# New numbers for the open experts before each search, fewer packed sums, and TensorE's order as written in the expert loop

## The chip, the cores and the metric

The kernel runs on one core of a Trainium2 chip. The metric is the device time of one execution in microseconds (us). A core has engines with an instruction stream each: TensorE (PE in the profile, its weight loads PEld), VectorE (DVE), ScalarE (ACT), GpSimd (POOL) and SyncE (SP), and 16 DMA engines that move data.

## The reference, cut to what matters

```python
y = irfft(rfft(x, axis=1) * (filt_r + 1j * filt_i), axis=1)       # x: 8 x 3072 x 256
t = y.reshape(24576, 256)
t = np.maximum(np.maximum(t @ w1, t @ w2), t @ w3) @ w_out        # first stage
logits = t @ w_gate                                               # 24576 x 8, second stage
for idx in argsort(-logits.flatten()):
    tok, e = idx // 8, idx % 8
    if assigned[tok] >= 0 or counts[e] >= 3072: continue          # 24576 / 8
    assigned[tok] = e; counts[e] += 1
for e in range(8):
    out[assigned == e] = relu(t[assigned == e] @ W1[e]) @ W2[e]    # 256 -> 1024 -> 256
```

Every expert ends with exactly 3072 tokens.

## The kernel before, in words

The filter and the first stage fill the time to about 2157 us of the profiled span and are not touched. The second stage never sorts. Each token claims the open expert on which its logit is greatest (`best` holds the logit, `code` the expert's number, 8 for expert 0 down to 1 for expert 7). The expert that is filled next is the one whose 3072nd-best claim is the highest, and its tokens are the claims above that threshold. `pick(j)` finds both. It searches the threshold bit by bit, from bit 30 down, with 33 counts in all; a count asks, for a trial threshold and all experts at once, how many claims reach it. The counts of three experts share one float32: `W[k]` holds, for each token, 1, 256 or 65536 by the expert that it claims, and one VectorE instruction (`ck`, line 828) makes the masked sum over a partition's 192 tokens. Three such sums make the eight counts. Two conversions (lines 833 and 834) take the packed words apart into bytes, a TensorE matmul with ones (line 836) adds the bytes over the partitions, and a compare (line 866) tells whether any expert reaches 3072. The next trial follows from it, so a search is a ring through VectorE and TensorE. Behind the search two small steps settle ties; `weights` starts the DMA of the found expert's weights and then splits them into high and low halves; `slots` turns the selection into token numbers: a running sum (line 703), three matmuls, and then six blocks of four matmuls each into two PSUM tiles `pg` (line 734), after which VectorE makes two masked sums for each tile (`jk`, line 744) and the numbers `ids` (line 748); a compare `G` (line 720) prepares the next block. `between(j)` is `clear(j)`, which takes the filled expert and its tokens out, and `prepare(j + 1)`, which makes the claims and the words `W` anew.

The work itself is a loop of 8 experts `j` by 48 steps `i`: six groups of 512 tokens by eight slices of the hidden layer. A step is six matmuls of 128x512 into `hq` (three products of float32 halves for each of two depths), a ScalarE relu `qh` (line 1016), a VectorE residual `ql` (line 1017), and, one step late, twelve matmuls of 128x256 into `yp`. Tokens come by indirect DMA, `gather`, are transposed on TensorE (`xt`, line 931, two times four transposes a group) and split into `xh` and `xl`; results leave by indirect DMA from GpSimd (line 961). `xt` and `pg` share one PSUM pool of two buffers. Line numbers 77 and 78 are the helper that splits into halves, 82 to 84 the helper that issues the three products.

The search and the slots for the next expert run beside an expert's steps. The generator `side` is advanced once a step: `pick(j + 1)` in steps 0 to 42, `between(j + 1)` from step 43 (`SWITCH`) on. Each `yield` in these functions is thus a step's end. In the first expert, `side` is the rest of the first pick, then `between(0)`, then `pick(1)`, and it is advanced twice in the steps 0 to 6. Ahead of the loop the string `START` advances the first weights (w), the first gather (g) and the first pick (s).

Where nothing else is said, a planner orders each engine's instructions by its own costs. Inside `tc.manual_schedule(engines=set(MAN))`, with `MAN` TensorE alone, TensorE takes its instructions in the order in which the program issues them. Before the change this holds for the part ahead of the loop, in which the first pick runs beside the last blocks of the first stage.

Of the kernel before, what the change touches and what calls it, by code (L numbers as in the profile page):

```python
# [59 lines left out]
E = 8  # L60
# [569 lines left out]
def phase2(tc, X2, M, first_claims, e8, Woh, Wol, H, wa, wb, pos16, tabs, ident, out):  # L630
# [4 lines left out]
    with ExitStack() as ctx:  # L635
# [38 lines left out]
        def small(n, name, dt=F32):  # L674
            return rp.tile([128, n], dt, tag=name, bufs=2, name=name)
# [25 lines left out]
        def slots(j, sel, rs):  # L701
            scan = rp.tile([128, NTT], F16, tag="scan", name=f"scan{j}")
            v.tensor_tensor_scan(
                out=scan, data0=one1.to_broadcast([128, NTT]), data1=sel, initial=0.0, op0=ALU.mult, op1=ALU.add
            )
            pd = ranks
            nc.tensor.matmul(pd[:, NTT : NTT + 1], shift, rs, start=True, stop=True)
            nc.tensor.matmul(pd[:, NTT + 2 : NTT + 3], tri, rs, start=True, stop=True)
# [41 lines left out]
                yield  # L750

        prep = {}
        loads = []
        chosen = {}

# [3 lines left out]
        def prepare(j):  # L759
            if j == E - 1:  # L760
                return
            m = best
            eq = rp.tile([128, NTT, E], F16, tag="eq", name=f"eq{j}")
            code = rp.tile([128, NTT], F32, tag="code", name=f"code{j}")
            for t in pieces():
                n = NTT // NS
                v.tensor_reduce(out=m[:, t], in_=M[:, t], axis=AX.X, op=ALU.max)
                v.scalar_tensor_tensor(out=m[:, t], in0=alive[:, t], scalar=-NEG, in1=m[:, t], op0=ALU.mult, op1=ALU.min)
                v.tensor_tensor(
                    out=eq[:, t], in0=M[:, t], in1=m[:, t].unsqueeze(2).to_broadcast([128, n, E]), op=ALU.is_equal  # L770
                )
                if NY > 1:
                    yield
                v.tensor_tensor(out=eq[:, t], in0=eq[:, t], in1=e8h.unsqueeze(1).to_broadcast([128, n, E]), op=ALU.mult)
                v.tensor_reduce(out=code[:, t], in_=eq[:, t], axis=AX.X, op=ALU.max)
                if NS < 4 or (t.start // (NTT // NS)) % 2:
                    yield
            W = rp.tile([128, 3, NTT], F32, tag="W", name=f"W{j}")
            for e in range(E):
                k, f = divmod(e, 3)  # L780
                dst = W[:, k, :]
                if f:
                    dst = rp.tile([128, NTT], F32, tag="pen", bufs=2, name=f"pen{j}_{e}")
                v.tensor_scalar(
                    out=dst, in0=code, scalar1=float(E - e), scalar2=float(256**f), op0=ALU.is_equal, op1=ALU.mult
                )
                if f:
                    v.tensor_tensor(out=W[:, k, :], in0=W[:, k, :], in1=dst, op=ALU.add)
            prep[j] = m, code, [W[:, k, :] for k in range(3)]
            yield  # L790

        def clear(j):
            if j == E - 1:
                return
            sel, oh = chosen.pop(j)
            v.scalar_tensor_tensor(out=alive, in0=sel, scalar=-2.0, in1=alive, op0=ALU.mult, op1=ALU.add)
            v.tensor_tensor(out=open_, in0=open_, in1=oh, op=ALU.subtract)
            v.tensor_scalar(out=oh, in0=oh, scalar1=2.0 * NEG, scalar2=-NEG, op0=ALU.mult, op1=ALU.add)
            for t in pieces():
                v.tensor_tensor(  # L800
                    out=M[:, t], in0=M[:, t], in1=oh.unsqueeze(1).to_broadcast([128, NTT // NS, E]), op=ALU.min
                )
            yield

        def pick(j):
            if j == E - 1:
# [12 lines left out]
                yield from slots(j, sel, rs)  # L819
                return  # L820
            m, code, W = prep.pop(j)

            def count(thr):

                pk = small(3, "pk")
                for k in range(3):
                    jk = rp.tile([128, NTT], F16, tag="ck", bufs=2, name=f"ck{j}")
                    v.scalar_tensor_tensor(
                        out=jk, in0=m, scalar=thr, in1=W[k], op0=ALU.is_ge, op1=ALU.mult,
                        accum_out=pk[:, k : k + 1],  # L830
                    )
# [5 lines left out]
                return ranks[:, :12]  # L837

# [12 lines left out]
            v.tensor_scalar(out=pos, in0=neg, scalar1=1, scalar2=None, op0=ALU.bitwise_xor)  # L851
            for b in range(30, -1, -1):
                pc = yield from count(tr.bitcast(F32))
                nx = small(1, "nx", I32)
                v.tensor_scalar(out=nx, in0=tr, scalar1=(1 << b) >> 1, scalar2=None, op0=ALU.bitwise_xor)
                met = small(1, "met", I32)
                v.scalar_tensor_tensor(
# [6 lines left out]
                hit = small(12, "hit")  # L864
                any_ = small(1, "any")
                v.tensor_scalar(
                    out=hit, in0=pc, scalar1=float(CAP), scalar2=0.0, op0=ALU.is_ge, op1=ALU.max, accum_out=any_
                )
                v.copy_predicated(out=tr, mask=any_.bitcast(I32), data=met)
            t2 = small(1, "tr", I32)  # L870
# [1 line left out]
            T = t2.bitcast(F32)  # L872
            pc = yield from count(T)
            full = small(12, "full")
            v.scalar_tensor_tensor(out=full, in0=pc, scalar=float(CAP), in1=e12, op0=ALU.is_ge, op1=ALU.mult)
            cs = small(1, "cs")
            v.tensor_reduce(out=cs, in_=full, axis=AX.X, op=ALU.max)
# [3 lines left out]
            v.tensor_scalar(out=est, in0=cs, scalar1=-1.0, scalar2=float(E), op0=ALU.mult, op1=ALU.add)  # L881
# [26 lines left out]
            loads.append(weights(j, est))  # L908
            yield from slots(j, sel, rs)
            chosen[j] = sel, oh  # L910

        last_store = [None]
        xs = {}
# [209 lines left out]
                    next(blocks, None)  # L1123
        drain(blocks)
        nxt = gather(0, 0)
        for act in START:
            if act == "w" and (0, 0) in xs and WB:
                with tc.issue_after(ready[0, 0].ins), tc.issue_after(rested[0].ins):
                    next(loads[0])
            elif act == "w" and (0, 0) in xs:  # L1130
                with tc.issue_after(rested[0].ins):
                    next(loads[0])
            elif act == "w":
                next(loads[0])
            elif act == "s":
                next(first_pick)
            else:
                next(nxt, None)
        units = steps()
        for j in range(E):  # L1140
            for i in range(6 * NF2):
                c, f = divmod(i, NF2)
                if i == 0:
                    side = iter(())
                    if j + 1 < E:
                        side = chain(first_pick, between(0), pick(1)) if j == 0 else pick(j + 1)
                if i < 6:
                    next(loads[0], None)
                if i == 7:
                    drain(loads.pop(0))  # L1150
                if i == SWITCH and j + 1 < E:
                    drain(side)
                    for _ in range(3 - began):
                        next(loads[0])
                    side = between(j + 1) if j + 2 < E else iter(())
                if j == 0 and i < 7 + S0:
                    next(side, None)
                if i < 7:
                    began = 0
                next(side, None)  # L1160
                if i >= 8 and loads and began < 3:
                    began += 1
                    next(loads[0])
                if c < 5 and f in (0, 4, 6):
                    if f == 0:
                        nxt = gather(j, c + 1)
                    next(nxt, None)
                if c == 5 and j + 1 < E and i >= SWITCH:
                    if i == SWITCH:
                        nxt = gather(j + 1, 0)  # L1170
                    if i != SWITCH + 1:
                        next(nxt, None)
                pump(post)
                next(units)
        drain(units)
        for p in post:
            for _ in p:
                pass
# [200 lines left out]
```

## Time and profile before

| | us |
|---|---|
| median of three timed runs | 3372.5 |
| lowest and highest | 3362.42, 3375.43 |
| the profiled execution | 3405.73 |
| its span | 3404.0 |
| TensorE busy in the span | 3247.4 |
| VectorE busy | 2178.8 |
| ScalarE busy | 1182.1 |
| GpSimd busy | 956.2 |

The span runs from the first to the last instruction of the profiled execution, which took 33 us longer than the median. The mean granted TensorE clock of it is 0.985 of full speed (2.4 GHz; the lower level is 1.2 GHz). A matmul is pipelined: the duration of a record reaches into the next one, so the time that it costs is read from the distance between starts.

### The profile page before, as it was taken

To read this page: it belongs to the slowest core of one execution; us is meant where nothing else is said; L and a number is where in the kernel's file an instruction comes from. 1 tells how busy PE (TensorE), PEld (TensorE's weight loads), DVE (VectorE), ACT (ScalarE), POOL (GpSimd) and SP (SyncE) were. 2 spreads that over 40 slices of the span, in tenths; PEclk is the share of its full clock that TensorE was granted. 3 is DMA by queue.
4 is the path that set the end of the run, shared out by engine and by line. 5 is a ranking of instruction groups with operands and counts; after the bars stand their busy time and mean duration, and the time that the engine had idled before them with its cause. 6 is when DMAs were issued, how large, how long until landed. Compare 5 with 4: busy or idle time off the path is not lost.

```text
span 3404.0 us, 51441 instructions
## 1 busy us (share of the span) xinstructions
PE 3247.4 (95%) x18447; PEld 2744.8 (81%) x18447; DVE 2178.8 (64%) x6518; ACT 1182.1 (35%) x2050; POOL 956.2 (28%) x877
## 2 busy tenths in 40 slices
PE   6799999999999999999999998799999999999999
PEld 3677877888888888888887878688788888888998
DVE  5876588557754477644444458888887878885222
ACT  3344355434433344422222224232222232323232
POOL 3542144113311123200000007324434342425332
PEclk8899999999999999999999999999999999999999
DMA  9655434523324323210112126211111111212110
GB/s 259 178 154 151 145 117 118 179 83 101 105 86 127 100 80 96 86 38 30 38 64 72 62 83 196 87 57 52 63 42 62 44 66 38 69 38 90 46 45 32
DMA packets 166015, 304.77 MB, mean 90 GB/s; under 512 B 22608, under 2 KB 66064, under 8 KB 163712
## 3 DMA queue, kind: packets, MB, share of 16 engines
q1 hardware_dynamic: 137392, 221.29, 21.1%
q0 software_dynamic: 28368, 80.20, 7.9%
q8 instruction: 145, 2.38, 0.3%
q14 instruction: 110, 0.90, 0.1%
HBM read 185.14 MB, written 116.39 MB: 89 GB/s over the span
## 4 chain that ended last, share of the span: by engine, by line
PE 82%; DVE 8%; DMA 4%; issue 3%; ACT 2%; POOL 1%; another core or an unknown queue 1%; SPq 0%; POOLq 0%; ACTq 0%; DVEq 0%
PE hp L84 11%; PE hp L83 11%; PE hp L82 11%; PE yp L82 5%; PE yp L84 5%; PE hq L84 5%; PE hq L82 5%; PE yp L83 5%; PE hq L83 5%; PE x2p L83 3%; PE x2p L82 3%; PE x2p L84 3%; PE s3p L467 2%; PE cc L82 2%; PE cc L83 2%
## 5 line engine op out<-in xcount | busy, mean ns | idle before, releaser
L503 DVE TENSOR_TENSOR h<-hp,h 128x512 f32<-128x512 f32 x576 | 397.7, 691 | 470.6 <-PE hp L84 464.9
L82 PE MATMUL hp<-x1h,Wh 128*128 128x512 f32 x1728 | 687.5, 398 | 6.3 <-ACT h L501 6.0
L83 PE MATMUL hp<-x1l,Wh 128*128 128x512 f32 x1728 | 683.2, 395 | 0.0
L84 PE MATMUL hp<-x1h,Wl 128*128 128x512 f32 x1728 | 682.4, 395 | 0.0
L1016 ACT ACTIVATE qh<-hq 128x512 fp32r<-128x512 f32 x376 | 224.5, 597 | 675.0 <-PE hq L84 516.8
L82 PE MATMUL yp<-w2h,qh 128*128 128x256 f32 x1504 | 434.7, 289 | 8.7 <-ACT qh L1016 6.3
L84 PE MATMUL yp<-w2h,ql 128*128 128x256 f32 x1504 | 432.7, 288 | 3.1 <-DVE ids L748 0.9
L83 PE MATMUL yp<-w2l,qh 128*128 128x256 f32 x1504 | 430.2, 286 | 0.0
L77 ACT CAST hh<-h 128x512 fp32r<-128x512 f32 x288 | 178.8, 621 | 661.4 <-DVE h L503 652.3
L1017 DVE SCALAR_TENSOR_TENSOR ql<-hq,qh 128x512 fp32r<-128x512 f32 x376 | 258.8, 688 | 221.6 <-ACT qh L1016 207.6
L82 PEld LDWEIGHTS hp<-x1h,Wh 128*128 128x128 f32 x1728 | 324.3, 188 | 88.1 <-ACT h L501 10.0
L84 PEld LDWEIGHTS hp<-x1h,Wl 128*128 128x128 f32 x1728 | 324.4, 188 | 78.3
L83 PEld LDWEIGHTS hp<-x1l,Wh 128*128 128x128 f32 x1728 | 324.7, 188 | 74.2
L78 DVE TENSOR_TENSOR hl<-h,hh 128x512 fp32r<-128x512 f32 x288 | 222.4, 772 | 213.9 <-ACT hh L77 213.7
L82 PE MATMUL hq<-xh,w1h 128*128 128x512 f32 x768 | 318.2, 415 | 1.6 <-ACT xh L77 1.6
L82 PEld LDWEIGHTS yp<-w2h,qh 128*128 128x128 f32 x1504 | 289.8, 193 | 32.4 <-ACT qh L1016 10.1
L83 PE MATMUL hq<-xl,w1h 128*128 128x512 f32 x768 | 309.2, 403 | 0.0
L84 PE MATMUL hq<-xh,w1l 128*128 128x512 f32 x768 | 306.2, 399 | 0.0
L83 PEld LDWEIGHTS yp<-w2l,qh 128*128 128x128 f32 x1504 | 289.8, 193 | 14.0 <-issue 1.9
L961 POOL DMA_INDIRECT out_dram<-ro,ids x188 | 185.3, 985 | 400.4 <-ACT ro L955 308.1
L84 PEld LDWEIGHTS yp<-w2h,ql 128*128 128x128 f32 x1504 | 290.1, 193 | 9.0 <-issue 4.5
L920 POOL DMA_INDIRECT gx<-X,ids x192 | 183.5, 956 | 343.6 <-PE xt L931 273.2
(248 smaller groups left out, 6254.6 us busy)
## 6 DMA issues: line engine op xcount, KB each, us to landing
xi<-in_x_dram SPq DMA_DIRECT2D x96, 256.0 KB, 3.6
z<-xo SPq DMA_DIRECT2D x96, 256.0 KB, 3.7
wi<-z SPq DMA_DIRECT2D x128, 192.0 KB, 2.6
z<-yo SPq DMA_DIRECT2D x128, 192.0 KB, 2.6
zi<-z SPq DMA_DIRECT2D x96, 256.0 KB, 2.8
X<-rows SPq DMA_DIRECT2D x38, 512.0 KB, 3.0
ft<-in_filt_dram SPq DMA_DIRECT2D x75, 256.0 KB, 4.0
H<-h SPq DMA_DIRECT2D x60, 256.0 KB, 2.0
```

Of the source, the lines that this page charges most:

```text
L77: nc.scalar.copy(hi, src)
L78: (lo_engine or nc.vector).tensor_tensor(out=lo, in0=src, in1=hi.bitcast(F32), op=ALU.subtract)
L82: nc.tensor.matmul(ps, ah, bh, start=start, stop=False)
L83: nc.tensor.matmul(ps, ah, bl, start=False, stop=False)
L84: nc.tensor.matmul(ps, al, bh, start=False, stop=stop)
L467: nc.tensor.matmul(ps[:, k, b * 128 : b * 128 + 128], zt[:, b * 256 + k * 128 : b * 256 + k * 128 + 128], ap[:, ns[b % len(ns)] % 2], star ...
L503: nc.vector.tensor_tensor(out=h, in0=ps, in1=cur, op=ALU.max)
L920: nc.gpsimd.indirect_dma_start(out=gt, out_offset=None, in_=X2, in_offset=bass.IndirectOffsetOnAxis(ap=ids[j][:, a : a + 1], axis=0))
L961: st = nc.gpsimd.indirect_dma_start(out=out, out_offset=bass.IndirectOffsetOnAxis(ap=ids[j][:, a : a + 1], axis=0), in_=ro[:, i, :], in_of ...
L1016: nc.scalar.activation(hh, ps, AF.Relu)
L1017: v.scalar_tensor_tensor(out=hl, in0=ps, scalar=0.0, in1=hh.bitcast(F32), op0=ALU.max, op1=ALU.subtract)
```

## The change

Ahead of each search but the first the open experts are numbered anew, from the number of those that are open down to 1, in the old order: a running sum over the eight flags `open_` gives the new numbers (`er[j]`, and `e8h` for the codes), `e12` is shifted by one. The words `W` for the search of pick `j` are then built for `8 - j` experts, so that there are three of them for picks 0 and 1, two for picks 2 to 4, and one for 5 and 6; `count` makes that many sums and carries that many words on. The winner's old number, which `weights` needs, comes back through one more masked sum (`jo`, `eo`). One search word (`nx`) and the selection (`sel`) now lie in the PSUM tile `bank`.

`slots` yields once more, behind its running sum. `between(0)` is issued ahead of the loop, by five letters b in `START`, and `side` is advanced twice in steps 0 to 4 of the first expert instead of 0 to 6. The whole expert loop and the last units stand under `tc.manual_schedule`, so TensorE takes the instructions of a step as written: those of `side` first, then transposes, then the six matmuls of `hq` and the twelve of `yp`.

```diff
-S0 = 0
+TWICE = 5
-START = "wgggwsw"
+START = "wgggwswbbbbb"
...
-        e12 = tb[:, 236:248]
+        e12 = cp.tile([128, 12], F32, name="e12")
+        v.tensor_copy(e12, tb[:, 236:248])
...
-        whole = bank[:, 508:511].bitcast(I32)
+        whole, turned = bank[:, 508:511].bitcast(I32), bank[:, 511:512].bitcast(I32)
...
 def slots(j, sel, rs):
     ...  # scan
+            yield
...
 def prepare(j):
-            for e in range(E):
+            for e in range(E - j):
...
-                    out=dst, in0=code, scalar1=float(E - e), scalar2=float(256**f), op0=ALU.is_equal, op1=ALU.mult
+                    out=dst, in0=code, scalar1=float(E - j - e), scalar2=float(256**f), op0=ALU.is_equal, op1=ALU.mult
...
-            prep[j] = m, code, [W[:, k, :] for k in range(3)]
+            prep[j] = m, code, [W[:, k, :] for k in range((E - j + 2) // 3)]
...
 def clear(j):
+            if j + 1 < E - 1:
+                n = E - 1 - j
+                pre = small(E, "pre")
+                v.tensor_tensor_scan(
+                    out=pre, data0=one1.to_broadcast([128, E]), data1=open_, initial=0.0, op0=ALU.mult, op1=ALU.add
+                )
+                v.tensor_scalar(out=pre, in0=pre, scalar1=-1.0, scalar2=float(n + 1), op0=ALU.mult, op1=ALU.add)
+                er[j + 1] = small(E, "er")
+                v.tensor_tensor(out=er[j + 1], in0=pre, in1=open_, op=ALU.mult)
+                v.tensor_copy(e8h, er[j + 1])
+                v.tensor_scalar(out=e12, in0=e12, scalar1=-1.0, scalar2=0.0, op0=ALU.add, op1=ALU.max)
...
 def pick(j):
+            nw = len(W)
-                for k in range(3):
+                for k in range(nw):
...
-                v.tensor_copy(whole, pk)
-                v.tensor_copy(by, whole.bitcast(U8))
+                v.tensor_copy(whole[:, :nw], pk[:, :nw])
+                v.tensor_copy(by[:, : 4 * nw], whole[:, :nw].bitcast(U8))
                 yield
-                nc.tensor.matmul(ranks[:, :12], ones, by, start=True, stop=True)
+                nc.tensor.matmul(ranks[:, : 4 * nw], ones, by[:, : 4 * nw], start=True, stop=True)
...
-                nx = small(1, "nx", I32)
+                nx = turned
...
-            v.tensor_scalar(out=oh, in0=e8, scalar1=cs, scalar2=None, op0=ALU.is_equal)
+            v.tensor_scalar(out=oh, in0=er[j], scalar1=cs, scalar2=None, op0=ALU.is_equal)
+            if j:
+                v.scalar_tensor_tensor(
+                    out=jo, in0=oh, scalar=1.0, in1=e8, op0=ALU.mult, op1=ALU.mult, accum_out=eo
+                )
+            else:
+                eo = cs
...
-            sel = rp.tile([128, NTT], F32, tag="sel", name=f"sel{j}")
+            sel = best
...
-                        side = chain(first_pick, between(0), pick(1)) if j == 0 else pick(j + 1)
+                            side = chain(first_pick, first_between, pick(1)) if j == 0 else pick(j + 1)
...
-                if j == 0 and i < 7 + S0:
+                    if j == 0 and i < TWICE:
...
+        with tc.manual_schedule(engines=set(MAN)):
             for j in range(E):
                 ...  # the loop over i as before
             drain(units)
```

## Rows read from the trace of the kernel before

**Rows 1.** The page, busy time, share of the span and instructions of each engine.

```profile
PE 3247.4 (95%) x18447; PEld 2744.8 (81%) x18447; DVE 2178.8 (64%) x6518; ACT 1182.1 (35%) x2050; POOL 956.2 (28%) x877
```

**Rows 2.** Windows over L1016, five searches: us from:to, length, ACT busy (x), PEclk, DMA, GB/s.

```profile
2322.00:2425.40 103.40, 19.71 (x33) 1.00 0.11 37
...
sum 513.70, ACT 98.73; mean ACT 19.75
```

**Rows 3.** The same view, the last 15 steps of experts 0 to 5.

```profile
2269.30:2322.00 52.70, 8.98 (x15) 1.00 0.27 91
...
3056.70:3115.20 58.50, 8.93 (x15) 0.91 0.35 118
sum 332.20, ACT 53.49; mean ACT 8.91
```

**Rows 4.** The same view: 33 steps of expert 7, 15 steps of expert 6.

```profile
3258.80:3355.60 96.80, 19.70 (x33) 1.00 0.12 39
3214.60:3258.80 44.20, 8.96 (x15) 1.00 0.16 48
```

**Rows 5.** TensorE's waits, 2161.6 to 3115 us: total us, times, longest us.

```profile
PE bank L836 <- DVE by L834: 12.0, 13, 1.1
PE pg L734 <- DVE ii L740: 10.8, 5, 3.3
PE pg L734 <- DVE ids L748: 7.0, 3, 4.0
PE yp L82 <- ACT qh L1016: 6.3, 2, 3.4
```

**Rows 6.** VectorE's instructions in one ring: start us, us, what, [idle before <-releaser].

```profile
2737.98 0.17 DVE L866 TENSOR_SCALAR_CACHE_REDUCE hit<-bank 128x12 f32<-128x12 f32 x1 [0.57 <-PE bank L836]
...
2738.45 0.42 DVE L828 SCALAR_TENSOR_TENSOR ck<-bank,tr,W 128x192 f16<-128x192 f32 x1
...
2739.47 0.68 DVE L1017 SCALAR_TENSOR_TENSOR ql<-hq,qh 128x512 fp32r<-128x512 f32 x1
2740.07 0.15 DVE L833 CAST bank<-pk 128x3 int32<-128x3 f32 x1
...
2740.26 0.17 DVE L834 CAST by<-bank 128x12 f16<-128x12 uint8 x1
...
2740.93 0.17 DVE L866 TENSOR_SCALAR_CACHE_REDUCE hit<-bank 128x12 f32<-128x12 f32 x1 [0.37 <-PE bank L836]
```

**Rows 7.** TensorE's instructions around the count matmul of that ring.

```profile
2740.70 0.18 PE L836 MATMUL bank<-by,sq 128*128 128x12 f16 x1
...
2740.94 0.28 PE L83 MATMUL yp<-w2l,qh 128*128 128x256 f32 x1
2741.06 0.28 PE L84 MATMUL yp<-w2h,ql 128*128 128x256 f32 x1
```

**Rows 8.** Groups of VectorE, 2161.6 to 3115.2 us: busy us, mean ns | idle before.

```profile
L828 DVE SCALAR_TENSOR_TENSOR ck<-bank,tr,W 128x192 f16<-128x192 f32 x576 | 209.6, 414 | 4.6
...
L720 DVE TENSOR_SCALAR G<-iota,base 128x512 f16<-128x512 int16 x36 | 17.7, 511 | 0.0
```

**Rows 9.** The chain of waits in expert 3's end: start us, us, what.

```profile
2749.07 5.74 DMA st<-in_moe_w_dram,ix
...
2759.12 0.47 PE pg L734 x2
```

**Rows 10.** ScalarE's first and ninth relu of expert 0.

```profile
2161.69 0.60 ACT L1016 ACTIVATE qh<-hq 128x512 fp32r<-128x512 f32 x1 [3.98 <-PE hq L84]
...
2189.98 0.60 ACT L1016 ACTIVATE qh<-hq 128x512 fp32r<-128x512 f32 x1 [1.04 <-DVE ck L828]
```

**Rows 11.** TensorE's waits, 2030 to 2161 us, ahead of the loop.

```profile
PE bank L836 <- DVE by L834: 12.6, 17, 0.9
PE xt L931 <- DMA gx<-X,ids: 8.7, 4, 7.1
```

More of the change, by code (lines that the diff above doesn't have):

```diff
@@ L752, in phase2 @@
         prep = {}
+        er = {0: e8}
         loads = []
@@ L866, in pick @@
                 v.tensor_scalar(
[L867 removed]
+                    out=hit[:, : 4 * nw], in0=pc, scalar1=float(CAP), scalar2=0.0, op0=ALU.is_ge, op1=ALU.max, accum_out=any_
                 )
@@ L874, in pick @@
             full = small(12, "full")
-            v.scalar_tensor_tensor(out=full, in0=pc, scalar=float(CAP), in1=e12, op0=ALU.is_ge, op1=ALU.mult)
+            v.scalar_tensor_tensor(
+                out=full[:, : 4 * nw], in0=pc, scalar=float(CAP), in1=e12[:, : 4 * nw], op0=ALU.is_ge, op1=ALU.mult
+            )
             cs = small(1, "cs")
-            v.tensor_reduce(out=cs, in_=full, axis=AX.X, op=ALU.max)
+            v.tensor_reduce(out=cs, in_=full[:, : 4 * nw], axis=AX.X, op=ALU.max)
             oh = bank[:, 500 : 500 + E]
-            v.tensor_scalar(out=oh, in0=e8, scalar1=cs, scalar2=None, op0=ALU.is_equal)
+            v.tensor_scalar(out=oh, in0=er[j], scalar1=cs, scalar2=None, op0=ALU.is_equal)
             est = small(1, "est")
-            v.tensor_scalar(out=est, in0=cs, scalar1=-1.0, scalar2=float(E), op0=ALU.mult, op1=ALU.add)
+            if j:
+                jo = small(E, "jo")
+                eo = small(1, "eo")
+                v.scalar_tensor_tensor(
+                    out=jo, in0=oh, scalar=1.0, in1=e8, op0=ALU.mult, op1=ALU.mult, accum_out=eo
+                )
+            else:
+                eo = cs
+            v.tensor_scalar(out=est, in0=eo, scalar1=-1.0, scalar2=float(E), op0=ALU.mult, op1=ALU.add)
             cm = rp.tile([128, NTT], F32, tag="cm", name=f"cm{j}")
@@ L908, in pick @@
             loads.append(weights(j, est))
+            chosen[j] = sel, oh
             yield from slots(j, sel, rs)
-            chosen[j] = sel, oh
         last_store = [None]
@@ L1125, in phase2 @@
         nxt = gather(0, 0)
+        first_between = between(0)
         for act in START:
@@ L1136, in phase2 @@
                 next(first_pick)
+            elif act == "b":
+                next(first_between, None)
             else:
@@ L1139, in phase2 @@
         units = steps()
[L1140 to L1145, printed above, removed]
-                        side = chain(first_pick, between(0), pick(1)) if j == 0 else pick(j + 1)
[L1147 to L1153, printed above, removed]
-                        next(loads[0])
-                    side = between(j + 1) if j + 2 < E else iter(())
-                if j == 0 and i < 7 + S0:
[L1157 to L1171, printed above, removed]
-                        next(nxt, None)
-                pump(post)
-                next(units)
@@ L1175, in phase2 @@
-        drain(units)
+        with tc.manual_schedule(engines=set(MAN)):
+            for j in range(E):
+                for i in range(6 * NF2):
+                    c, f = divmod(i, NF2)
+                    if i == 0:
+                        side = iter(())
+                        if j + 1 < E:
+                            side = chain(first_pick, first_between, pick(1)) if j == 0 else pick(j + 1)
+                    if i < 6:
+                        next(loads[0], None)
+                    if i == 7:
+                        drain(loads.pop(0))
+                    if i == SWITCH and j + 1 < E:
+                        drain(side)
+                        for _ in range(3 - began):
+                            next(loads[0])
+                        side = between(j + 1) if j + 2 < E else iter(())
+                    if j == 0 and i < TWICE:
+                        next(side, None)
+                    if i < 7:
+                        began = 0
+                    next(side, None)
+                    if i >= 8 and loads and began < 3:
+                        began += 1
+                        next(loads[0])
+                    if c < 5 and f in (0, 4, 6):
+                        if f == 0:
+                            nxt = gather(j, c + 1)
+                        next(nxt, None)
+                    if c == 5 and j + 1 < E and i >= SWITCH:
+                        if i == SWITCH:
+                            nxt = gather(j + 1, 0)
+                        if i != SWITCH + 1:
+                            next(nxt, None)
+                    pump(post)
+                    next(units)
+            drain(units)
```

2 lines of the change are left out of this document (1 added, 1 removed).

## The prediction

> **What bounds the kernel now.** I read the page first: TensorE is busy 95% of the profiled span [rows 1], so a microsecond is gained only where TensorE waits, runs at its lower clock, or loses work. The change touches the second stage alone (from about 2157 us on), so next I cut that stage by its own beat: line 1016, one ScalarE relu a step, 48 steps an expert. Windows over that line give the time of 33 or of 15 steps. The 33 steps of experts 1 to 5 in which the next expert is searched take 513.7 us in all, 103.4 us in the first of them and 102.7 in the mean [rows 2]. The same 33 steps of expert 7, which searches nothing, take 96.8 us, and the last 15 steps of expert 6, beside which nothing is picked, 44.2 us [rows 4]. The last 15 steps of experts 0 to 5, in which a search ends, its token numbers (slots) are made and the next tables are prepared, take 332.2 us in all [rows 3]. So the searches cost 513.7 - 5 x 96.8 = 29.7 us and the six ends 332.2 - 6 x 44.2 = 67.0 us over bare matmuls.
>
> Part of this is TensorE work that stays. A count and the matmul behind it take 0.24 us where a matmul alone takes 0.12 us [rows 7], so a count costs 0.12 us: 33 x 5 x 0.12 = 19.8 us, which leaves 9.9 us of stall in five searches. The 24 slot matmuls of a search are bounded by the same 0.12 us, 17 us in six ends; about 50 us of stall is left there. The list of waits agrees: TensorE waits 12.0 us for count bytes (13 times, 1.1 us at most), 10.8 + 7.0 us with slot matmuls for VectorE, 6.3 us for the relu [rows 5]. The rest of the ends is lower clock: the last end ran at a granted 0.91 (of 2.4 GHz; the other level is 1.2 GHz), the first at 1.00 [rows 3]. 9% of 58.5 us is 5.3 us, so 0 to 5.3 us an end; with the mean of the two, 2.65, that is about 16 us in six. 10.8 + 7.0 + 6.3 + 16 = 40 of the 50 us.
>
> The search itself is a ring: count matmul, VectorE's compare, masked sums, bytes, next count. The compare starts 0.23 us after its matmul [rows 6, 7]. From the compare at 2737.98 to the end of the bytes at 2740.26 + 0.17 it is 2.45 us, of which one residual of the experts' own work holds VectorE from 2739.47 to 2740.07, 0.6 us [rows 6]. So a ring takes 2.7 us, or 2.1 us alone. A search step of 102.7 us / 33 is 3.1 us: the ring hides in most steps.
>
> **The change, part by part.**
>
> Fewer sums. With new numbers the searches for experts 2, 3 and 4 pack six, five and four open experts in two sums, those for 5 and 6 in one. 33 counts each: 3 x 33 + 2 x 2 x 33 = 231 sums go. One is 0.41 us [rows 8], but three of them fill the time from 2738.45 to 2739.47, 0.34 us each [rows 6]: some 79 us of VectorE. It is hidden behind the step's own matmuls and worth nothing by itself; cover gone, it would be worth the 9.9 us of search stall. The mean wait is 12.0 / 13 = 0.92 us [rows 5]; a ring shorter by 0.34 us (two sums) or 0.68 us (one) leaves a third of that or so. I take -7 us, bounds 0 and -9.9. The search for expert 1 keeps three sums.
>
> Preparing tables loses 21 compares and 14 adds in all, each taken at no more than a sum: at most 14 us, off the path. Added are five operations on 8 or 12 columns after each search and one or two to get the expert's true number back. The nearest row is the compare on 12 columns, 0.17 us [rows 6]: below 1.2 us a search, beside 2.8 us of matmuls, so 0; if VectorE is late there, at most 6 x 1.2 = 7 us. The selection and one search word move to PSUM, where sums already read PSUM at 0.41 us [rows 8]; 0, with a bound of one short operation a count either way.
>
> Written order. In the main loop TensorE now takes, each step: the matmul of the search or the four of a slot block, then transposes, six first-layer matmuls, twelve second-layer ones. Today slot matmuls stand inside those groups and wait with the group behind them: 17.8 us [rows 5]. At the step's front, one step behind the VectorE work they need (the new yield puts the scan a step earlier too), their wait should go. Two slot tiles and two transpose tiles share two PSUM buffers. In the one step of a search in which a transpose follows the slots of the same step, it waits until a slot tile is read, two masked sums of 0.41 us plus small ones, some 1.0 us: +6 us in six searches. Of the 16 us of lower clock I let half go with the waits: -8, for no row says how much hangs on them. The end together: -17.8 + 6 - 8 = -20 us. Bounds: 0, if the waits only move, and -40, if all named above go.
>
> What speaks against this order: where it is already written, beside the last blocks of stage one, TensorE waits for count bytes 17 times in 33 counts, 12.6 us [rows 11], and nothing passes it. By the Trainium skill, page "TensorE: Matmul & The Clock Gate", section "Step-by-step: what each phase is for", matmuls stay in program order and only weight loads are pulled ahead; the 17 waits agree with it. By it the sum is that of the last rival below; by the rows of the ends it is the -20 us above.
>
> The start. Clearing and preparing for expert 1 are issued ahead of the loop (five b's), VectorE work that sits in the time in which TensorE waits for the first tokens, 7.1 us at once [rows 11]; 0. The two calls a step shrink from seven steps to five. In written order such pairs stand next to each other on TensorE: two pairs of slot blocks and two pairs of counts, each second one waiting for a VectorE pass of about 2.1 us (the ring alone). 4 x 2.1 = 8.4 us. Today the first eight steps take from 2161.69 to 2189.98 us, 28.3 us [rows 10], against 8 x 96.8 / 33 = 23.5: 4.8 us are lost already. Net +4; I take +5, bounds 0 and +9.
>
> Sum: -7 - 20 + 5 = -22 us on the profiled execution of 3405.7 us. The timed median is 33 us below that, so I apply the difference: 3372.5 - 22 = 3350 us, 0.65% faster.
>
> **The rivals.** (1) No change, within 0.5%. In the chain of waits of expert 3's end, 5.74 us are the next weights' transfer, on which ScalarE waits in line before the relu; the residual follows, and the slot matmul comes only at 2759.12 [rows 9]. And TensorE waits 6.3 us for relus outright [rows 5]. Neither is a matter of TensorE's order: what it wants next is that relu. Then the ends gain nothing and pay +6, and with -7 and +5 the time is 3372.5 + 4 = 3377 us. That the planner's order was already near the written one (3.1 us a search step) leads to the same. Against it: the slot waits are the larger sum, and they hold first-layer matmuls that need no relu.
>
> (2) Slower. Held in order, TensorE waits for each VectorE pass that outlasts its step. A slot step asks of VectorE four sums of 0.41, a residual of 0.6, one reach of 0.51 [rows 8] and small ones of some 0.25: 3.0 us, against 2.8 + 4 x 0.12 = 3.3 us of matmuls; with a transposed tile's residual (0.6) it is over. If the six slot steps and five preparing steps each wait 0.6 us, that is 11 x 0.6 x 6 = 40 us, +9 at the start, -7 in the search and -17.8 of present waits: +24, 3396 us. It decides from the point where the pass is longer than the step's matmuls. For it: [rows 11] and VectorE's load; against it: half of these steps have 0.3 us to spare.
>
> **How the numbers follow.** 0.5% of 3372.5 is 17 us, about what a measurement here can tell. The forecast (end waits shrink by 15 us or more) has 0.50, rival 1 has 0.27, rival 2 has 0.23: faster 0.50, same 0.27, slower 0.23. The forecast's own range goes from -50 us (search -9.9, end -40, start 0), 3322, to the edge at 3356. Eight in ten reach to rival 2's 3396: 3322 to 3396. The predicted time is the forecast's 3350.
>
> **What would show it.** Right: 33 search steps of experts 2 to 5 at 101 us or less (96.8 + 4) and no wait of counts for bytes there; slot matmuls in fours ahead of the first layer, waits below 1 us, ends near 52 us and granted clocks of 0.97 or more. The search for expert 1 keeps its waits, and the first eight steps take 31 to 34 us. Rival 1 shows as ends of 55 us with the relu as TensorE's releaser; rival 2 as slot matmuls or transposes released by VectorE in nearly every step. The prediction is wrong if the ends stay although the slot waits are gone, or if the 33 us between profile and median lie in those ends, so that timed runs have less to gain than the profile shows.

## The result

The change makes the kernel slower: 3421.4 us in the median against 3369.5, a ratio of 1.0149 (95% interval 1.0119 to 1.0179), some 52 us. Two repeats gave 1.0144 (1.0127 to 1.0161) and 1.0161 (1.0144 to 1.0179). The prediction had 3350 us and a range of 3322 to 3396, so both the sign and the range missed.

The page of the kernel after, its first lines:

```profile
span 3422.0 us, 50979 instructions
...
PE 3253.1 (95%) x18447; PEld 2768.4 (81%) x18447; DVE 2170.7 (63%) x6064; ACT 1183.8 (35%) x2050; POOL 956.2 (28%) x877
```

VectorE has 454 instructions fewer than in [rows 1], and TensorE is as busy. Windows over the relu (now line 1042), columns as in [rows 2]. First the searches of experts 1 to 5, which answer to [rows 2]:

```profile
2349.90:2449.80 99.90, 19.77 (x33) 1.00 0.12 38
...
sum 499.50, ACT 98.80; mean ACT 19.76
```

The six ends, which answer to [rows 3]:

```profile
2288.20:2349.90 61.70, 8.97 (x15) 0.92 0.22 76
...
3072.10:3128.90 56.80, 8.98 (x15) 0.94 0.36 121
sum 341.20, ACT 53.89; mean ACT 8.98
```

Expert 0's first 8 steps, its steps 8 to 33, and expert 6's first 8:

```profile
2166.90:2204.10 37.20, 4.79 (x8) 0.86 0.09 26
2204.10:2288.20 84.10, 14.97 (x25) 1.00 0.11 34
3128.90:3159.60 30.70, 4.80 (x8) 1.00 0.11 35
```

TensorE's waits from 2140 us to the end, columns as in [rows 5]:

```profile
PE pg L736 <- DVE ids L750: 17.0, 19, 3.2
PE xt L957 <- issue: 12.4, 2, 10.8
PE bank L852 <- DVE by L850: 10.2, 23, 2.4
PE xt L957 <- DVE ids L750: 9.4, 7, 1.9
PE xt L957 <- DMA gx<-X,ids: 9.1, 4, 7.0
PE pg L736 <- DVE xl L78: 7.5, 6, 2.8
PE yp L84 <- DVE ql L1043: 4.5, 7, 1.9
```

The searches came out as forecast, 99.9 us each and without a wait for count bytes (those of the list lie in expert 0 and ahead of it). The ends did not shrink, expert 0 takes 183 us where it took 160, and slot matmuls and transposes wait for VectorE's token numbers.

One thing must be known to read the sizes. Both profiles together show a loss of 18 us only, because the profile that the prediction rests on is 33 us longer than the timed runs of the kernel before. That goes with the chip, as the first experiment shows. On two chips the kernel before takes 3366 to 3369 us ("first kind" below), on another one 3401 us ("second kind"). What differs in them is not known.

### The profile page after: what moved, and what is told of

It reads as the page before. It is cut to its first block, busy times and chain, and to the rows that moved or that the text cites. A ratio compares the mean times of both kernels' runs of the same rounds, so it can differ in the third digit from the quotient of the medians.

```text
span 3422.0 us, 50979 instructions
## 1 busy us (share of the span) xinstructions
PE 3253.1 (95%) x18447; PEld 2768.4 (81%) x18447; DVE 2170.7 (63%) x6064; ACT 1183.8 (35%) x2050; POOL 956.2 (28%) x877
## 4 chain that ended last, share of the span: by engine, by line
PE 77%; DVE 10%; issue 6%; DMA 4%; ACT 2%; POOL 1%; SPq 0%; POOLq 0%; DVEq 0%; ACTq 0%
PE hp L83 11%; PE hp L84 11%; PE hp L82 11%; PE hq L82 5%; PE hq L83 4%; PE hq L84 4%; PE yp L83 4%; PE yp L82 4%; PE yp L84 4%; PE x2p L83 3%; PE x2p L84 3%; PE x2p L82 3%; PE s3p L467 2%; PE cc L82 2%; DMA ft<-in_filt_dram 2%
## 5 line engine op out<-in xcount | busy, mean ns | idle before, releaser
L82 PE MATMUL yp<-w2h,qh 128*128 128x256 f32 x1504 | 426.6, 284 | 0.5 <-ACT qh L1042 0.3
L82 PE MATMUL hq<-xh,w1h 128*128 128x512 f32 x768 | 330.5, 430 | 0.0
```

What stands on the lines that cost most here:

```text
L82: nc.tensor.matmul(ps, ah, bh, start=start, stop=False)
```

## The experiments

### The same kernels on both kinds of chip

No edit; both kernels profiled again.

> The kernel before, unchanged, profiled once more. The first profile took 3405.7 us while the timed runs have a median of 3369. Theory A: the extra 34 us lie in the ends of the searches, where the first profile shows relus released 3 to 8 us late, so a profile near 3370 us has ends of experts 0 to 5 (15 steps each) that take about 298 us in all instead of 332, searches as before (513.7 us for 33 steps of experts 1 to 5), and its ends are then shorter than those of the kernel after (341 us). Rival: the extra lies in the first stage (the second stage then starts about 34 us earlier, and its stages are as in the first profile), or this profile is at 3405 us again.

> The kernel before, unchanged: a profile is wanted from an execution near 3369 us, for both so far (3394 and 3406 us) are from one near 3400. Theory A: the 30 us are stalls in the ends of the searches (relus and slot sums released 3 to 8 us late), so the six ends of such an execution take about 300 us, where the two profiles show 327 and 332 and the kernel after 339 to 341; with them the loss of the change is 340 - 300 = 40 us in the ends, 17 in expert 0's first 33 steps, 9 in the start and -13 in the searches. Rival: the ends are as before and the 30 us are in the first stage, ahead of the first relu at 2157 to 2162 us.

> The kernel after, unchanged, timed beside the kernel before on another chip. On the chip of the first three tests the kernel before took 3401 us where it took 3369 on that of the result. If the loss is in the work of the second stage (the two profiles differ there by 1110 - 1091 = 19 us, by 29 us with what lies ahead of it), it is 15 to 30 us here, 0.5 to 0.9%; rival: it is 52 us (1.5%) wherever it is measured, and the profile of before hides 33 us.

> The kernel before, unchanged, for a profile near 3369 us. Theory A: such an execution has none of ScalarE's waits for an unseen releaser (20 to 22 us in the profiles so far), its six ends take 300 us or less, and the rest is as in the earlier profiles. Rival: the ends take 327 to 333 us again and the time is lost or won ahead of 2157 us.

> The kernel after, unchanged, beside the kernel before on the chip of this call. If the chip is of the kind on which the kernel before takes 3400 us: by the three-sum run there (3493 us, of which 77 us of the second stage are not in the kernel after) 3417 us, or 0.5% above before. On the other kind 3419 us, 1.4% above, as twice before.

Measured: before_again 3394.5 us and before_third 3406.1 on the second kind (timed runs there: 3401.2), before_fourth 3370.8 on the first (3366.2). The kernel after took 3419.2 and 3420.8 us, both times on the first kind; it was not run on the second.

The expectation of 300 us or less for the six ends on the first kind was missed; they take 314.2 us there.

The two kinds can be told apart in the profile. ScalarE's waits, and the GpSimd queue's gathers with the time from issue to landing, on the second kind (before_third):

```profile
ACT qh L1016 <- remote: 20.1, 4, 8.1
```
```profile
gx<-X,ids POOLq DMA_INDIRECT x188
```

and the gathers on the first (before_fourth):

```profile
gx<-X,ids POOLq DMA_INDIRECT x188, 2.8
```

On the second kind ScalarE waits 20 us for a releaser that the trace does not show ("remote"), and the gathers' landings can't be followed; on the first there is no such wait. Every profile on the chip of the second kind lacks the landings; the wait is not in every one (6.7 us in before_written, none in before_written2), and whether it has a part in the 30 us is open. The profile behind [rows 1] to [rows 11] has the marks of the second kind, the timed runs the times of the first. The windows of before_fourth: expert 0's first 8 steps, its steps 8 to 33, expert 6's first 8:

```profile
2160.40:2186.40 26.00, 4.80 (x9) 0.98 0.21 62
2186.40:2262.70 76.30, 14.92 (x25) 1.00 0.11 36
3080.50:3106.50 26.00, 4.76 (x8) 1.00 0.12 39
```

its five searches and six ends, summed:

```profile
sum 503.60, ACT 98.68; mean ACT 19.74
...
sum 314.20, ACT 53.73; mean ACT 8.96
```

and the same of after_third, beside it on the same chip:

```profile
2165.50:2202.10 36.60, 4.78 (x8) 0.87 0.08 24
2202.10:2286.40 84.30, 14.98 (x26) 1.00 0.11 33
3126.70:3159.00 32.30, 4.80 (x9) 0.95 0.10 33
...
sum 499.50, ACT 98.46; mean ACT 19.69
...
sum 340.80, ACT 53.82; mean ACT 8.97
```

This gives the whole loss by stage: to the first relu 2165.5 - 2160.4 = 5.1 us; expert 0's first eight steps 10.6 and its search 8.0; the searches of experts 1 to 5 give back 4.1; the six ends cost 26.6; expert 6's first eight steps 6.3. The sum is 52.5 us, and the spans are 3369.0 and 3421.5 us.

### The order

```diff
-        with tc.manual_schedule(engines=set(MAN)):
+        if True:
```

for after_planner and after_planner2, at the head of the expert loop; before_written, before_written2 and before_written3 are the kernel before with that line added.

> The kernel after, with TensorE's order in the expert loop left to the planner. Theory A (the written order is what costs: TensorE stands behind late relus, residuals and slot sums): most of the loss goes, 3355 to 3375 us. Rival (the new start, the extra yield, the numbering and the PSUM tiles cost, the order does not): it stays at 3405 to 3425 us.

> The kernel after in the planner's order, beside the two others. It was 5 us above the kernel before where that took 3401 us. Theory A (the written order loses what the planner's order gains on the faster kind of chip): within 10 us of the kernel before here too, 3365 to 3380 us on the faster kind. Rival (the new numbers, the extra yield or the start lose it): 3400 us or more on the faster kind.

> The kernel before, with the expert loop under the written TensorE order and nothing else changed: three sums for every count. Theory A: the order alone costs more than the whole change, for the searches of experts 2 to 6 then run at the 3.39 us a step that the three-sum search beside expert 0 shows in the kernel after (against 3.02 us with fewer sums): 3421 + 5 x 33 x 0.35 = about 3480 us, at least 3440. Rival: the order is harmless and the time is that of before, 3360 to 3385 us.

> The kernel before under the written order alone, once more, beside the other two: it took 3411 us where the kernel before took 3401. If what makes the kernel before 30 us faster on some chips is lost by the written order, it takes 3411 us on a chip where the kernel before takes 3369; rival: it is 10 us above the kernel before on each chip.

> The kernel before under the written order and nothing else; 10 us above the kernel before on the slower kind of chip. Theory A: on the faster kind the order costs what it costs the rest of the change there, less the 8 us that the search word adds with it: 30 to 40 us, 3395 to 3410 us, in the start, the first eight steps of expert 0 and the six ends. Rival: 10 us here too, and the loss of 41 us needs the rest of the change.

Measured: after_planner 3406.4 us on the second kind, 1.0013 of before (1.0003 to 1.0023). after_planner2 3379.7 on the first kind, 1.0047 (1.0032 to 1.0063). The three before_written, all on the second kind, 3411.0, 3410.4 and 3410.7, 1.0027 to 1.0028; what the order alone costs on the first kind was thus not measured.

Beside after_third on the same chip, the written order costs 3420.8 - 3379.7 = 41 us of the 54.6. By the stages of the two profiles it is 9.5 us to the first relu (2156.0 against 2165.5), 10.2 in expert 0's first eight steps, 8.4 in its search, 7.7 in the six ends (333.1 against 340.8) and 4.8 in expert 6's first eight steps: 40.6, as the spans (3421.5 and 3380.9). So only 7.7 of the 26.6 us that the ends lose against before_fourth are the order's; 18.9 are lost in the planner's order too (after_planner2, the six ends):

```profile
sum 333.10, ACT 53.56; mean ACT 8.93
```

The five searches take 499.5 us in either order. The first of the losses in after_third, TensorE's slot matmuls ahead of the first hq:

```profile
2154.84 1.08 PE L736 MATMUL pg<-rhs,G 128*128 128x194 f16 x4 [1.19 <-DVE xl L78]
...
2161.63 0.50 PE L736 MATMUL pg<-rhs,G 128*128 128x194 f16 x2 [3.18 <-DVE ids L750]
```

Twelve slot matmuls stand ahead of the first step, each block waiting until VectorE has read the one before; in the wait of 3.18 us VectorE makes the tables `W` for expert 1, from 2157.57 to 2160.22. That before_written costs 10 us and not 80 says that the three-sum ring is no slower under the written order by itself; the expectation of 3480 us was wrong, and the ring's delay needs another part of the change.

### The sums and the search word

after_threesums keeps the new numbers but makes three sums always (words without experts hold zeros); after_nx puts the search word back into SBUF.

```diff
-            prep[j] = m, code, [W[:, k, :] for k in range((E - j + 2) // 3)]
+            prep[j] = m, code, [W[:, k, :] for k in range(3)]     # after_threesums
...
-                nx = turned
+                nx = small(1, "nx", I32)                          # after_nx
```

> The kernel after, but every count makes three sums (words without experts are zeros); numbering, order and start as in after. If in the written order the ring through VectorE and TensorE sets the step, each of the 165 search steps beside experts 1 to 5 is 0.35 us longer: 3421 + 58 = about 3480 us. Rival: the sums are hidden beside the matmuls as in the kernel before, and the time is 3421 + at most 10 us.

> The kernel after with the search word nx in SBUF as before; everything else of the change stays. Theory A: in the bank's tile the word waits for the count matmul, so three short VectorE operations and a wait of 0.26 us that ran beside it stand in the ring; without that the three-sum search beside expert 0 falls from 3.36 to 3.04 us a step, its steps 8 to 33 from 84.1 to about 76 us and the first eight from 37 to about 34: 9 to 12 us less than the kernel after; the searches of two and one sums stay at 99.9 us. Rival: what lengthens expert 0's steps is the order itself, and the time is that of after.

Measured: after_threesums 3493.4 us, 1.0269 (1.0251 to 1.0287), on the second kind; its five searches take 558.3 us where those of the kernel after take 499.5 (on the first kind). after_nx 3412.5 us where after_again took 3419.2; expert 0's steps 8 to 33 take 76.0 us instead of 84.2. The five searches of after_threesums:

```profile
sum 558.30, ACT 98.63; mean ACT 19.73
```

Expert 0's steps 8 to 33 of after_nx:

```profile
2200.60:2276.60 76.00, 14.98 (x25) 1.00 0.12 37
```

So three sums are too long for a step in the kernel after, and hidden in before_written (its five searches take 503). What makes the difference in expert 0's search is the word, together with the written order: with the word in PSUM and the planner's order (after_planner2) those steps take 75.9 us. VectorE in expert 0's search, after_third:

```profile
2236.56 0.69 DVE L1043 SCALAR_TENSOR_TENSOR ql<-hq,qh 128x512 fp32r<-128x512 f32 x1 [0.21 <-ACT qh L1042]
2237.17 0.15 DVE L849 CAST bank<-pk 128x3 int32<-128x3 f32 x1
2237.36 0.17 DVE L850 CAST by<-bank 128x12 f16<-128x12 uint8 x1
2237.78 0.16 DVE L871 TENSOR_SCALAR bank<-tr 128x1 int32<-128x1 int32 x1 [0.26 <-PE bank L852]
2237.98 0.16 DVE L873 SCALAR_TENSOR_TENSOR met<-neg,bank 128x1 int32<-128x1 int32 x1
2238.06 0.15 DVE L877 SCALAR_TENSOR_TENSOR tr<-pos,bank 128x1 int32<-128x1 int32 x1
2238.12 0.16 DVE L882 TENSOR_SCALAR_CACHE_REDUCE hit<-bank 128x12 f32<-128x12 f32 x1
```

The word (line 871) waits for the count matmul, for both write the tile bank, and it and the two operations that need it stand for 0.34 us ahead of the compare, from 2237.78 to 2238.12; in the kernel before they run between the sums and the compare, beside the matmul (before_fourth):

```profile
2237.55 0.15 DVE L855 TENSOR_SCALAR nx<-tr 128x1 int32<-128x1 int32 x1
...
2238.55 0.17 DVE L866 TENSOR_SCALAR_CACHE_REDUCE hit<-bank 128x12 f32<-128x12 f32 x1 [0.50 <-PE bank L836]
```

The residual ql stands in the ring in both, as it does in [rows 6]; in after_nx it runs behind the conversions, while the count matmul is awaited. The Trainium skill, page "PSUM — Partial Sum Buffer", section "PSUM bank collisions raise a hardware error", says that PSUM has to be guarded by bank, in the simple form of its rule, and not by address. The wait of 0.26 us behind a matmul on other columns of the bank agrees with it.

### The start, the slot compares, and three edits at once

```diff
-TWICE = 5
-START = "wgggwswbbbbb"
+TWICE = 7
+START = "wgggwsw"                                                 # after_start
...
-            G = rp.tile([128, CAP], F16, tag="G", name=f"G{j}")
+                Gs[c] = rp.tile([128, 512], F16, tag="G", bufs=2, name=f"G{j}_{c}")   # after_reach
```

after_three has both and the search word in SBUF.

> The kernel after with the start of before: nothing of between(0) ahead of the loop, two calls a step in steps 0 to 6. Theory A: half of the loss ahead of the first relu goes (slot blocks no longer wait for VectorE's tables; the last transposes to the first relu take 5 instead of 12 us) and the end of expert 0 is some 4 us shorter, 8 to 12 us less than after. Rival: the pairs in written order cost the same wherever the tables are made, or cost more in seven steps than in five: after, or up to 8 us more.

> The kernel after with the slot compares G in two small buffers instead of one long tile, so that VectorE can't make all six ahead of the first slot sums. In the kernel after the six compares beside GpSimd's weight splits take 10.6 us in expert 0's end and 6 to 7 in the others, where one alone takes 0.33 us. Theory A: that stretch is what TensorE waits for, and the six ends get shorter by 3 us each or more, 18 us in all, so that the time is at or below that of the kernel before. Rival: whichever VectorE operation stands beside GpSimd's splits is stretched, or the late relu behind the weights' transfer decides; the ends stay within 1 us each.

> The kernel after with three edits at once: the search word in SBUF, the start of before, the slot compares in two buffers; written order and new numbers stay. By the single runs (-6.6, -8 and -2 us) it takes 3419 - 17 = 3402 us where the kernel before takes 3369, and 3402 where that takes 3400. Theory A: what is left of the loss is the written order's. Rival: the three were the loss and it comes to the time of the kernel before.

Measured: after_start 3411.0 us, 8.2 below after_again; the first relu comes at 2160.4 instead of 2166.0, and expert 0's end takes 54.2 us instead of 63.4. after_reach 3417.5 us, 1.7 below, which is no difference: expert 0's end falls by 6 us, the other five stay (275.7 against 275.3), and the expected 18 us did not come. after_three 3430.2 us, where 3402 was expected, 1.0093 (1.0076 to 1.0110), on the second kind; 29 us above the kernel before, where the kernel after is 50 above it on the first kind. That fits the sum of the three, but across kinds of chip it proves nothing.

### The numbers alone

numbers_only is the kernel before with the new numbers, the extra yield in slots and the selection in PSUM, but the planner's order, the old start and the search word in SBUF. fewer_sums leaves out the yield and the place of the selection as well:

```diff
-            yield
...
-            sel = best
+            sel = rp.tile([128, NTT], F32, tag="sel", name=f"sel{j}")
```

> The kernel before with the new numbers and the fewer sums alone (the planner's order, the start of before, the search word in SBUF; the extra yield and the selection in PSUM stay). Theory A (the sums are hidden behind the matmuls, and the loss is the order's and the start's): within 10 us of the kernel before, the searches beside experts 1 to 5 some 10 us shorter in all. Rival (numbering, yield or the selection in PSUM cost at the ends): 15 us or more above the kernel before.

> The kernel before with the new numbers and fewer sums and nothing else of the change (planner's order, the start of before, selection and search word in SBUF, no extra yield). Theory A: the sums were hidden, so 0 to 5 us less than the kernel before, by the 0.5 us for each of five searches that the searches beside experts 1 to 5 take less in the kernel after, and some VectorE work less in the ends. Rival: the planner, given fewer sums, places the slot work worse in the ends, and it takes 5 to 10 us more than the kernel before.

> fewer_sums plus the extra yield and the selection in PSUM. It was 4.5 us above the kernel before on a chip of the slower kind. Of the 13.5 us by which the kernel after in the planner's order is above the kernel before on the faster kind, 11 are in expert 0's end and thus the start's. Theory A: 0 to 6 us above the kernel before. Rival: the yield and the selection in PSUM carry them, and it is 10 us or more above.

Measured, all on the second kind: numbers_only 3405.7 and numbers_only2 3403.7 us, 1.0014 (1.0002 to 1.0025) and 1.0009 (0.9997 to 1.0021). fewer_sums 3377.7, 0.9931 (0.9917 to 0.9944): 23 us faster than the kernel before, where 0 to 5 were expected, and the yield with the place of the selection costs 26.0 us again. By the profiles of fewer_sums and numbers_only2, 24.4 of them are in the six ends. Those of fewer_sums:

```profile
sum 318.80, ACT 53.49; mean ACT 8.92
```

and of numbers_only2:

```profile
sum 343.20, ACT 53.77; mean ACT 8.96
```

The profile of numbers_only, the same kernel, came out 10 us shorter than its median, with 333.2 us in the ends, so the share of the ends is known to some 10 us. The two edits were not tried apart.

The ends show a reason why it is the yield. VectorE's slot compares and GpSimd's weight splits in expert 3's end of fewer_sums:

```profile
2736.52 1.67 DVE L721 TENSOR_SCALAR G<-iota,base 128x512 f16<-128x512 int16 x6
...
2738.08 3.73 POOL L78 TENSOR_TENSOR w1l<-st,w1h 128x512 fp32r<-128x512 f32 x3 [1.75 <-ACT w1h L77]
```

and of numbers_only2:

```profile
2755.77 0.69 DVE L1043 SCALAR_TENSOR_TENSOR ql<-hq,qh 128x512 fp32r<-128x512 f32 x1 [5.20 <-ACT qh L1042]
...
2756.97 1.03 DVE L722 TENSOR_SCALAR G<-iota,base 128x512 f16<-128x512 int16 x1
2758.53 3.33 DVE L722 TENSOR_SCALAR G<-iota,base 128x512 f16<-128x512 int16 x3
...
2755.33 5.11 POOL L78 TENSOR_TENSOR w1l<-st,w1h 128x512 fp32r<-128x512 f32 x4 [2.31 <-ACT w1h L77]
2760.40 5.16 POOL L78 TENSOR_TENSOR w2l<-st,w2h 128x512 fp32r<-128x512 f32 x4
```

Six compares take 1.67 us when all but the last are made before the splits begin. One step later they stand behind the residual ql, which waits 5.20 us for a relu that is itself behind the weights' transfer (ScalarE waits 4.78 us for it); so they fall beside the splits and take 0.8 to 1.3 us each. The residual at 2761.79, beside the same splits, keeps its 0.68 us. The selection's own instruction takes 0.37 us in PSUM and 0.36 in SBUF. All 42 compares of the expert loop in fewer_sums (total us, mean ns, idle us before them):

```profile
L721 DVE TENSOR_SCALAR G<-iota,base 128x512 f16<-128x512 int16 x42 | 13.4, 383 | 0.0
```

and in numbers_only2:

```profile
L722 DVE TENSOR_SCALAR G<-iota,base 128x512 f16<-128x512 int16 x42 | 40.0, 986 | 0.0
```

They take 21.4 us in before_fourth and 44.6 in after_third. The difference of 26.6 us is about that of the two times, but compare time is not lost time one for one: after_reach took 9.2 us off the compares (36.8 against 46.0 in after_again) and 1.7 off the kernel.

In after_third's first end the stretch is longest, two compares beside seven splits and then TensorE's transposes:

```profile
2293.71 8.87 DVE L722 TENSOR_SCALAR G<-iota,base 128x512 f16<-128x512 int16 x2
...
2293.58 4.93 POOL L78 TENSOR_TENSOR w1l<-st,w1h 128x512 fp32r<-128x512 f32 x4
2298.48 3.69 POOL L78 TENSOR_TENSOR w2l<-st,w2h 128x512 fp32r<-128x512 f32 x3
...
2303.96 1.09 PE L957 MATMUL xt<-ident,gx 128*128 128x128 f32 x4 [10.04 <-issue]
```

The trace names no releaser for the 10.04 us ("issue"); the buffer that the transposes need is read by VectorE behind those compares. The splits keep their 1.23 us each; VectorE gets through when GpSimd stops. The Trainium skill, page "SBUF — State Buffer", section "SBUF: two separate sides", says that VectorE in its fast modes and GpSimd share a port pair that one of them holds for a whole instruction; the rows agree, and show that back-to-back GpSimd work can hold VectorE off for several instructions.

## Why the prediction was wrong

**What bounds the kernel.** That TensorE's idle time is what counts was right. The sizes came from a profile of the second kind of chip: the six ends take 332.2 us there and 314.2 on the first kind, whose times the timed runs have, so not 50 but 32 us of stall lay over bare and slot matmuls. The prediction named this case at its end, that the 33 us between profile and median lie in the ends; 18 of them do, and 9 in the searches of experts 1 to 5 (512.8 us in before_third, 503.6 in before_fourth). It still subtracted the gains from the median.

**Fewer sums.** -7 us, bounds 0 and -9.9, was near for the searches as profiled: they fall by 10.6, from 512.8 us in before_third to 502.2 in fewer_sums, a little past the bound. The ends fall by 14.4 with them (333.2 to 318.8), for which the prediction had nothing; why was not tried. On the first kind TensorE does not wait for count bytes in the kernel before at all, and the searches of after_third give 4 us.

**Search word and selection in PSUM at 0.** This step failed for the word: the price is not in the operation but in the wait for the matmul that writes the same bank, which in the written order puts the word into the ring. It costs 6.7 us by the times (after_again less after_nx), 8 in expert 0's search. With fewer sums the ring is short enough again, so the two edits partly pay each other. The bound of one short operation a count did not hold: a wait of 0.26 us and three operations entered the ring.

**The ends at -20 us.** This step failed by the most, 46.6 of the 74.5 us between the forecast of -22 and the 52.5 of the two profiles: the six ends lose 26.6 us (314.2 in before_fourth, 340.8 in after_third). The prediction let the waits of the slot matmuls go (17.8 us, of which 3.1 are in expert 0's first eight steps and not in the ends) because these would stand one step behind the VectorE work that they need. They do not: VectorE is late in the ends, behind relus that wait for the weights (ScalarE waits 22.1 us for these transfers in before_fourth and 25.3 in after_third) and with stretched compares, and in the written order the slot matmuls and the transposes at the step's front hold all 18 matmuls of the step. In the six ends TensorE's waits with slot matmuls fall only from 18.2 to 12.8 us, where -17.8 was taken, and those with transposes rise from none to 17.7, where +6 was taken. The granted clock, from which -8 us was taken, went the other way: 0.89 to 0.97 in the six ends of after_third, 0.94 to 1.00 in those of before_fourth. Only 7.7 of the 26.6 us are the order's; the rest stays in the planner's order.

**The extra yield counted as a gain.** The prediction took it as help for the slot matmuls' waits. It moved the slot compares beside GpSimd's splits. Together with the selection's place it costs 26 us on the second kind, most of it in the ends. The two were not separated by a run; the compares' place in the traces speaks for the yield, and on the first kind no run has it alone.

**The start at +5, bounds 0 and +9.** After_third loses 5.1 us to the first relu and 10.6 in the first eight steps, past the bound; 19.7 us there are the order's, about half of the 41 that it costs in all. 8.2 of the loss in the start and in expert 0's end is the early tables with the five paired steps (after_start), which the prediction took as free beside TensorE's wait for tokens: the slot sums of the first expert wait behind the tables on VectorE.

**Not foreseen:** expert 6's first eight steps, 6.3 us, in which the last expert's slots run without a search ahead of them; 4.8 of them are the order's.

**The rivals.** The first (ends unchanged, 3377 us) is near the kernel after in the planner's order, 3379.7, but by luck: the ends of that run are 18.9 us longer. The second, slot matmuls and transposes that wait in order for VectorE, was nearest to the truth in kind, and the range ended at its price; it spread 40 us of waits evenly over 11 steps of each end, had 9 us for the start, where 15.7 were lost, and not the stretched compares.

fewer_sums is the version to keep from the change: faster than the kernel before, where both were measured, by 0.7%. On the first kind of chip it was not run.

## What to carry to other kernels

Compare the profile's own time with the timed runs before anything else, and where they differ by more than the gain that is forecast, take no stall from that profile as certain. An order written by hand gave something only in searches that still had waits (512.8 us in before_third, 503 in before_written; 499.5 either way with fewer sums) and hurt where a wait varies: whatever waits at a step's front holds the whole step. A scratch word in a PSUM bank that a matmul of the same loop writes can put that matmul's wait into the ring, and a step moved by one yield has to be priced by what runs beside it on the other engines.

## What the runs showed of the hardware that was not expected

The same kernel takes 3366 to 3369 us on two chips and 3401 us on a third, at the same mean granted clock (0.985 in before_fourth and in before_third); on the third the landings of GpSimd's transfers are missing from the trace and ScalarE waits 20 us for an unseen releaser. A VectorE compare of 128x512 that takes 0.28 us among its like (1.67 / 6) takes 4.4 us in the mean of two beside GpSimd's back-to-back subtractions (8.87 / 2), which keep their 1.23 us. A residual of the same size, which reads one operand from PSUM, is not stretched beside them (0.68 us).
